# Attention's feature products in 64-column halves, two logits tiles, and a new order for late pieces: linear attention with two MoE layers

## The chip, the cores and the metric

The kernel runs on one core of a Trainium2 chip. The metric is the device time of one execution in microseconds, the median of several runs. The engines are named as in the profile: PE is TensorE, DVE VectorE, ACT ScalarE, POOL GpSimd, SP the engine that issues most DMAs.

## The reference

Three layers follow each other on 1152 tokens (batch 2 x 576 positions) of width 512. The first is linear attention with random features, 8 heads of 64 and 128 features; the second is a feed-forward layer with a clipped activation, whose weights come in 64-bit floats; the third sends each token to the best of 8 experts, at most 288 tokens to each.

```
def phi(x):
    h = einsum('bhsd,md->bhsm', x, omega) - sum(x * x) / 2
    return exp(h - max(h)) / sqrt(m)
kv  = einsum('bhsm,bhsd->bhmd', phi(k), v);  z = sum_s phi(k)
out = einsum('bhsm,bhmd->bhsd', phi(q), kv) / (phi(q) . z + 1e-6)

h = x @ w_in;  y = (h * clip(h + 3, 0, 6) / 6) @ w_out

expert_idx = argmax(y @ w_gate)        # top 1, softmax weight gate_w
out[i] = gate_w[i] * (relu(y[i] @ w1[e]) @ w2[e])   # first 288 tokens of e, others 0
```

## The kernel before

**Attention.** Work is cut into 18 units, listed in `seq`: eight of the keys, eight of the queries (batch x half of the positions x group of heads), and a rest unit of each (`R`, the last 64 positions of both batches). A unit has eight slots of 128 positions, in two halves of four. Its steps have letters: XH and XL split the input into a high and a low part (ScalarE, then GpSimd or VectorE, `halve_x`); B makes the features `pj` on TensorE (`features`, L792); N is the maximum on VectorE (`nm`, L798); P the exponentials on ScalarE (`phi`, L804, one instruction a slot). Key units then do K, `kv_acc`: one product a slot with `phi` as the 128 x 128 stationary operand and 65 columns of the values (`kvp`, L815), accumulated over the four units of a batch. Query units do C and T (`turn_phi`: `tpC` on TensorE, L845, copied to `phT` on ScalarE, L849), D (`attend`: `nd`, four slots a half, L863), R, S, X on VectorE (division), E (`turn_out`: `tpE`, L888), EH and EL (copy and low part of `xT`, L911 and L914). The rest unit's `nd` (L861) already goes in two 64-column halves, since its two batches need different `kvz`.

**First MoE layer.** Each of 16 blocks f of w_in and of w_out arrives as 512 KB of 64-bit words and is turned into 32-bit floats by five operations (L245 to L255): for all blocks in `abs_act` the first is on ScalarE, the others on VectorE. For w_in, ScalarE copies the high part (`wsplit`, L261) and GpSimd subtracts it (L263). The hidden groups `hp` (`hidden_in`, L276, twelve products of 384 columns, 48 groups: 16 f x 3 groups of tokens g) follow, then `t` (ScalarE, L280), `g` (VectorE, L284) and a store to DRAM. The gate is folded into w_out: `tpW` turns a w_out block (L298), `wogp` multiplies it with w_gate (L308). The logits `lg` (`logits`, L330) add `wog` (8 columns) times `g` over f, the three token groups at column tiles 0, 32 and 64 of one bank. In the last six f (`TAIL`) the steps are for token group 0 alone, then for 1 and 2. `logits_out` copies them (`lc`), `turn_logits` turns them (`lgr`, L352 and L355).

**Experts.** The first expert is chosen from the first 384 tokens while the hidden layer still runs. A window of tokens is loaded (`gw`), halved (`gh` on ScalarE L564, the low part on VectorE L566), and multiplied with halved w_out (`yw`, L573) into `dT` (L583 and L585), the input of the expert. The expert's weights arrive in eight loads (`rawe`: four of w1, L605, four of w2, L608) and each is split into two halves, 16 in all (`wsplit`, L618 on ScalarE, then L620 on VectorE and GpSimd in turn); `hp` (L641) is its first product.

**The order.** A planner adds each step with its engine, an estimated cost, a rank, what it comes `after`, and what buffers it `takes` and `frees` (`tp`: four PSUM banks, `pj` two, `acc` one). It simulates the engines, and `DELTA` moves attention's steps by numbers. What comes out is a fixed row of instructions for each engine, which the chip runs in that row; the costs have no other effect. DMA issues on SP are such a row too.

## Time and profile before

| | |
|---|---|
| median of 3 runs | 341.66 us (340.96 to 342.4) |
| profiled execution | 339.61 us, span 337.7 us |
| PE busy | 319.2 us, 95% |
| DVE busy | 226.5 us, 67% |
| ACT busy | 177.7 us, 53% |
| POOL busy | 75.3 us, 22% |

The span goes from the first to the last instruction; the rest of the device time lies around it. Attention's products take about the first 82 us, the first MoE layer runs to 214, the entry of the first expert to 246.5. Busy shares are means over stages with different limits, so the rows further down are by stretch.

### The profile page before, as it was taken

The page shows a single profiled execution, that of the slowest core. Times are in us where ns is not written, and L with a number is a line of the kernel's source. Part 1 is how long each engine was busy: PE and PEld are TensorE (multiplying, and loading weights), DVE is VectorE, ACT ScalarE, POOL GpSimd, SP SyncE. Part 2 cuts the span into 40 slices and gives each one's busy share as a digit, 9 for nine tenths or more (in the row PEclk, how much of TensorE's full clock was granted, in tenths as well). Part 3 has the DMA queues.
Part 4 walks back from the last instruction along what each step waited for, and adds up shares of the span by engine and source line. Part 5 has one row for each costly group of instructions (what it writes and reads, how often), then busy time and mean ns, then how long its engine had stood idle before and what let it go on. Part 6 is the DMA issues. An engine that isn't in the chain of part 4 may idle for free.

```text
span 337.7 us, 6444 instructions
## 1 busy us (share of the span) xinstructions
PE 319.2 (95%) x2311; PEld 291.3 (86%) x2311; DVE 226.5 (67%) x466; ACT 177.7 (53%) x428; POOL 75.3 (22%) x74
## 2 busy tenths in 40 slices
PE   7999899999999998999899999989889999999992
PEld 5999899999989895979687888789789989999782
DVE  5589999898899899979988634269857002835100
ACT  5988899982445464555478223343727132633110
POOL 0755643100131033013100000033406012601021
PEclk9999999999999999999999999999979999999998
DMA  7997940004756868885533142781963006600011
GB/s 247 351 338 271 310 158 32 34 2 171 209 186 214 274 219 258 244 267 199 180 140 118 47 147 73 233 285 45 307 194 127 2 22 186 229 3 0 4 47 31
DMA packets 29673, 54.06 MB, mean 160 GB/s; under 512 B 5536, under 2 KB 18208, under 8 KB 29632
## 3 DMA queue, kind: packets, MB, share of 16 engines
q1 hardware_dynamic: 29248, 52.38, 47.1%
q0 software_dynamic: 384, 1.18, 1.1%
q8 instruction: 20, 0.33, 0.4%
q14 instruction: 21, 0.17, 0.2%
HBM read 37.42 MB, written 16.13 MB: 159 GB/s over the span
## 4 chain that ended last, share of the span: by engine, by line
PE 51%; DMA 16%; DVE 15%; issue 12%; ACT 3%; SPq 1%; POOL 1%; POOLq 0%; ACTq 0%; DVEq 0%
PE hp L276 13%; PE yw L573 8%; PE hp L641 6%; DMA raw<-in_w_in_dram 6%; PE pj L792 6%; PE yq L663 4%; PE nd L863 4%; DMA raw<-in_w_out_dram 4%; PE lg L330 3%; DMA rawe<-in_w_dram 2%; DVE g L284 2%; DVE x L255 2%; PE kvp L815 2%; PE tpC L845 2%; DVE x L253 2%
## 5 line engine op out<-in xcount | busy, mean ns | idle before, releaser
L276 PE MATMUL hp<-xT,wsplit 128*128 128x384 f32 x576 | 107.8, 340 | 0.0
L276 PEld LDWEIGHTS hp<-xT,wsplit 128*128 128x128 f32 x576 | 98.9, 188 | 6.1 <-issue 5.3
L573 PE MATMUL yw<-gh,ohi 128*128 128x288 f32 x256 | 52.1, 298 | 0.2 <-ACT scratch L703 0.2
L280 ACT ACTIVATE t<-hp,three 128x384 f32<-128x384 f32 x48 | 27.7, 578 | 39.2 <-PE hp L276 38.0
L620 POOL TENSOR_TENSOR wsplit<-rawe,wsplit 128x512 fp32r<-128x512 f32 x16 | 22.3, 1394 | 102.2 <-ACT wsplit L618 101.9
L804 ACT ACTIVATE phi<-pj,nm 128x128 f32<-128x128 f32 x144 | 40.6, 415 | 5.9 <-DVE nm L798 4.9
L573 PEld LDWEIGHTS yw<-gh,ohi 128*128 128x128 f32 x256 | 40.9, 188 | 1.6 <-issue 0.6
L263 POOL TENSOR_TENSOR wsplit<-x,wsplit 128x512 fp32r<-128x512 f32 x16 | 21.8, 1360 | 90.3 <-ACT wsplit L261 87.0
L284 DVE SCALAR_TENSOR_TENSOR g<-t,hp 128x384 f32<-128x384 f32 x48 | 26.3, 549 | 19.1 <-ACT t L280 19.0
L566 DVE TENSOR_TENSOR gh<-gw,gh 128x288 fp32r<-128x288 f32 x32 | 19.6, 624 | 29.0 <-ACT gh L564 29.0
L573 PE MATMUL yw<-gh,olo 128*128 128x288 f32 x128 | 37.6, 294 | 0.0
L641 PE MATMUL hp<-dT,wsplit 128*128 128x288 f32 x192 | 27.8, 307 | 3.0 <-DVE dT L585 2.2
L641 PEld LDWEIGHTS hp<-dT,wsplit 128*128 128x128 f32 x192 | 27.2, 198 | 3.2 <-DVE dT L585 2.5
L798 DVE TENSOR_REDUCE nm<-pj 128x4 f32<-128x512 f32 x36 | 24.6, 684 | 4.8 <-PE pj L792 4.0
L782 POOL TENSOR_TENSOR xl<-rawx,xh 128x512 fp32r<-128x512 f32 x16 | 21.6, 1359 | 24.1 <-ACT xh L780 24.1
L792 PE MATMUL pj<-wbd,xh 128*128 128x256 f32 x144 | 25.6, 300 | 1.4 <-ACT xh L780 1.0
L573 PEld LDWEIGHTS yw<-gh,olo 128*128 128x128 f32 x128 | 24.1, 189 | 0.0
L618 ACT ACTIVATE wsplit<-rawe 128x512 fp32r<-128x512 f32 x32 | 19.0, 623 | 8.5 <-DMA rawe<-in_w_dram 8.4
L792 PEld LDWEIGHTS pj<-wbd,xh 128*128 128x128 f32 x144 | 19.5, 190 | 3.2 <-ACT xh L780 2.1
L564 ACT ACTIVATE gh<-gw 128x288 fp32r<-128x288 f32 x32 | 13.5, 438 | 14.1 <-PE yw L573 10.7
L620 DVE TENSOR_TENSOR wsplit<-rawe,wsplit 128x512 fp32r<-128x512 f32 x16 | 16.5, 1031 | 4.2 <-ACT wsplit L618 4.0
L253 DVE SCALAR_TENSOR_TENSOR x<-raw,x 128x512 int32<-128x512 int32 x16 | 18.7, 1170 | 0.4
(150 smaller groups left out, 481.5 us busy)
## 6 DMA issues: line engine op xcount, KB each, us to landing
gall<-g SPq DMA_DIRECT2D x48, 192.0 KB, 2.4
...
```

The source lines that it names most:

```text
L253: nc.vector.scalar_tensor_tensor(out=x, in0=lw, scalar=29, in1=x, op0=ALU.logical_shift_right, op1=ALU.bitwise_or)
L263: nc.gpsimd.tensor_tensor(out=t[:, 1, :], in0=xf, in1=t[:, 0, :].bitcast(F32), op=ALU.subtract)
L276: nc.tensor.matmul(hp, lhsT=w[:, a, wk], rhs=xT[g][b_][:, kk, :], start=(n == 0), stop=(n == 3 * KD - 1))
L280: nc.scalar.activation(out=t, in_=hp, func=ACTF.Relu, bias=three[:, 0:1])
L284: nc.vector.scalar_tensor_tensor(out=gv, in0=t, scalar=6.0, in1=hp, op0=ALU.min, op1=ALU.mult)
L573: nc.tensor.matmul(self.ps[kk], lhsT=wohalf[f][a][:, kk * 128:(kk + 1) * 128], rhs=self.gh[f][:, b_, :], start=(f == YORDER[0] and n == 0) ...
L620: engine.tensor_tensor(out=lo, in0=part, in1=hi.bitcast(F32), op=ALU.subtract)
L641: nc.tensor.matmul(hp, lhsT=self.w[0, f][:, a, kk * 128:(kk + 1) * 128], rhs=self.window.dT[b_][:, kk, :], start=(n == 0), stop=(n == 3 * ...
L782: (nc.gpsimd if u in X_POOL else nc.vector).tensor_tensor(out=lo[:, sl], in0=rawt[u][:, sl], in1=hi[:, sl].bitcast(F32), op=ALU.subtract)
L792: nc.tensor.matmul(pj[:, 2 * jj:2 * jj + 2, :], lhsT=a[:, j, :], rhs=w, start=(jj == 0 and n == 0), stop=(n == 2), skip_group_check=True,)
L798: nc.vector.tensor_reduce(out=nm, in_=pj, axis=AX.X, op=ALU.max, negate=True)
L804: nc.scalar.activation(out=phis[u][:, 4 * half + h, :], in_=pj[:, h, :], func=ACTF.Exp, bias=nm[:, h:h + 1])
```

## The change

Five things are changed.

1. `kv_acc` takes a whole unit in one step, and each slot's product is made in two halves of 64 columns of `phi` (`CH`), which land in partitions 0 to 63 and 64 to 127. `attend_products` does the same for `nd`: one step D0 a unit of sixteen products, with two `tp` banks taken at once, after both `phT` halves. `C` of a unit comes after D0 of the unit two before it.
2. `DELTA` has other numbers, the planner some other costs, and hidden groups from the seventh on come after all of attention.
3. For the eight late w_in blocks (`abs_act`, f 8 to 15) the low part of `wsplit` is subtracted on VectorE in place of GpSimd.
4. `wog` has 32 columns. In the tail the odd f of a pair goes to another column tile (3, 0 and 3 for groups 0, 1 and 2), so that two rows of weights are worked on at once; `summed` adds the two tiles when the logits are turned. The copy is one for all 128 partitions in each of the two parts, the first turning is now three products like the second, and the clearing of the scratch (`lz`) is gone.
5. The first expert's loads go out as w2 0 to 2, w1 0 to 3, w2 3, the first three without waiting for the window loads. The save of the second part's `meta` comes after the last window load.

```
-        nc.gpsimd.tensor_tensor(out=t[:, 1, :], in0=xf, in1=t[:, 0, :].bitcast(F32), op=ALU.subtract)
+        (nc.vector if key in abs_act else nc.gpsimd).tensor_tensor(out=t[:, 1, :], in0=xf, in1=t[:, 0, :].bitcast(F32), op=ALU.subtract)
...
-        wog[b] = const.tile([128, BLOCK, E], F32, name=f"wog{b}")
-        nc.scalar.activation(out=wog[b], in_=tp[:, :, 0:E], func=ACTF.Copy)
+        wog[b] = const.tile([128, BLOCK, 32], F32, name=f"wog{b}")
+        nc.scalar.activation(out=wog[b], in_=tp, func=ACTF.Copy)
...
         for f in fs:
             for g in gs:
+                other = f % 2 > 0 and len(gs) < NG
+                ct = {0: 3, 1: 0, 2: 3}[g] if other else g
                 nc.tensor.matmul(
-                    lg[0][32 * g:32 * g + E, :], lhsT=wog[f // BLOCK][:, f % BLOCK, :], rhs=gt[f, g],
-                    start=(f == 0), stop=(f == F1T - 1), skip_group_check=True,
+                    lg[0][32 * ct:32 * ct + 32, :], lhsT=wog[f // BLOCK][:, f % BLOCK, :], rhs=gt[f, g],
+                    start=(f == 0 or (other > 0 and f == F1T - TAIL + 1)), stop=(f >= F1T - PAIR), skip_group_check=True,
                 )
...
-    def logits_out(g):
-        ps = slice(32 * g, 32 * g + E)
-        nc.scalar.activation(out=lgT[0][ps], in_=lg[0][ps], func=ACTF.Copy)
+    def logits_out(p):
+        if not p:
+            lgT[0] = scratch()[:, 0:GT]
+        nc.scalar.activation(out=lgT[0], in_=lg[0], func=ACTF.Copy)
...
-        if p == 0:
-            for c in range(TPG):
-                nc.tensor.transpose(lgr[p][:, c, :], lgT[0][0:E, c * 128:(c + 1) * 128], ident[0:E, 0:E])
-            return
         for c in range(TPG):
-            nc.tensor.matmul(
-                lgr[p][:, c::TPG, :], lhsT=lgT[0][:, c * 128:(c + 1) * 128],
-                rhs=ident.rearrange("p (g e) -> p g e", e=32)[:, 1:NG, 0:E], start=True, stop=True,
-            )
+            nc.tensor.matmul(lgr[p][:, c::TPG, :], lhsT=lgT[0][:, c * 128:(c + 1) * 128], rhs=summed[:, p:2 * p + 1], start=True, stop=True)
...
+        for g, (a, b) in enumerate(((0, 3), (1, 0), (2, 3))):
+            nc.gpsimd.tensor_tensor(out=summed[:, g], in0=tiles[:, a], in1=tiles[:, b], op=ALU.add)
...
+    def kv_acc(b, u, first, last):
...
+        for s in range(8):
             h, r = slot_head(u, s)
-            nc.tensor.matmul(
-                kv_ps[b][:, h, r:r + D + 1], lhsT=phis[u][:, s, :], rhs=vt[:, h, r * (D + 1):(r + 1) * (D + 1)],
-                start=first and s == 0, stop=last, skip_group_check=True,
-            )
+            for c in CH:
+                nc.tensor.matmul(
+                    kv_ps[b][c, h, r:r + D + 1], lhsT=phis[u][:, s, c], rhs=vt[:, h, r * (D + 1):(r + 1) * (D + 1)],
+                    start=first and s == 0, stop=last, skip_group_check=True,
+                )
...
+    def attend_products(u):
+        b = seq[u][1]
+        phT = phTs[u]
+        for half in range(2):
+            nds[u, half] = pt.tile([128, 4, 128], F32, tag="tp", name="nd")
+        for s in range(8):
+            h, r = slot_head(u, s)
+            for n, c in enumerate(CH):
+                nc.tensor.matmul(nds[u, s // 4][c, s % 4, 0:D + 1], lhsT=phT[:, s, c], rhs=kvz[n if b == "R" else b][:, h, 1:D + 2])
...
+        plan.add(
+            f"D0{u}", "PE", 1.2, lambda u=u: attend_products(u), after=[f"T0{u}", f"T1{u}"] + [f"KV{bb}" for bb in range(B) if b in (bb, "R")],
+            takes=[("tp", f"D{z}{u}") for z in range(2)], frees=[f"T0{u}"], rank=rank("D", u))
...
-            (f"H{me}", "PE", 2.09, dict(after=[f"WLi{f}"] + rows_of(g), takes=tag, frees=[f"wi{f}"] + ([f"x{g}0", f"x{g}1"] if f == F1T - 1 else []), rank=n)),
+            (f"H{me}", "PE", 2.09, dict(after=[f"WLi{f}"] + rows_of(g) + (attended if n >= 6 else []), takes=tag, frees=[f"wi{f}"] + ([f"x{g}0", f"x{g}1"] if f == F1T - 1 else []), rank=n)),
...
+        if k == 0:
+            parts = parts[F2T // 2:-1] + parts[:F2T // 2] + parts[-1:]
+        for n, (kind, h) in enumerate(parts):
+            early = k == 0 and n < F2T // 2 - 1
+            load2(f"e{k}.{kind}{h}", lambda a=(kind, h): x.load(*a), 2.0, 2.5, after=[f"ce{k}"] + ([] if early else [f"Lgw{k}.{min(F1T - 1, 4 * n + 3 - 10 * (k == 0))}"]), takes="raww", rank=-1900 + n + 400 * k,
```

How the rows of instructions move, at three places. An entry is a line of the kernel (two or three lines off between the two), an operation, its output and inputs and its shape; names are those of the code.

TensorE, the end of attention, before: the last `nd` groups, each of a half unit, stand in a row with `tpE` and `tpC`, and the first hidden group (L276) follows.

```order
L792 MATMUL pj<-wbd_140,xh 128x256 x2
L792 MATMUL pj<-wbd_141,xh 128x256 x2
L792 MATMUL pj<-wbd_140,xl 128x256 x2
L861 MATMUL nd<-kvz,phT 64x65 x8
L863 MATMUL nd<-kvz,phT 128x65 x8
L888 MATMUL tpE<-ident,x 128x128 x4
L845 MATMUL tpC<-ident,phi 128x128 x8
L888 MATMUL tpE<-ident,x 128x128 x4
L276 MATMUL hp<-xT_93,wsplit 128x384
```

The same place after, from the last but two `tpE` on:

```order
L891 MATMUL tpE<-ident,x 128x128 x4
L847 MATMUL tpC<-ident,phi 128x128 x4
L790 MATMUL pj<-wbd_141,xh 128x256 x2
L790 MATMUL pj<-wbd_142,xh 128x256 x2
L790 MATMUL pj<-wbd_141,xl 128x256 x2
L863 MATMUL nd<-kvz,phT 64x65 x16
L847 MATMUL tpC<-ident,phi 128x128 x4
L277 MATMUL hp<-xT_94,wsplit 128x384
```

A unit's `nd` is one row of sixteen products (L863), behind the features of the last unit, and a hidden group (L277) stands behind the next `tpC`. Some rows later, where that hidden group ends:

```order
L277 MATMUL hp<-xT_94,wsplit 128x384
L891 MATMUL tpE<-ident,x 128x128 x4
L847 MATMUL tpC<-ident,phi 128x128 x4
L863 MATMUL nd<-kvz,phT 64x65 x32
L277 MATMUL hp<-xT_96,wsplit 128x384
```

The last two units' `nd` (32 products) follow the last `tpC`, and another hidden group stands ahead of the last `tpE`; three hidden groups stand before it in this stretch, two before the change.

VectorE, where a late block of w_in is decoded (`x_` with a number), before:

```order
L284 SCALAR_TENSOR_TENSOR g<-t,hp 128x384
L249 TENSOR_SCALAR x_1709<-x_1709 128x512
L251 TENSOR_SCALAR x_1709<-x_1709 128x512
L253 SCALAR_TENSOR_TENSOR x_1709<-raw,x_1709 128x512
L284 SCALAR_TENSOR_TENSOR g<-t,hp 128x384
L255 SCALAR_TENSOR_TENSOR x_1709<-raw,x_1709 128x512
L249 TENSOR_SCALAR x_1749<-x_1749 128x512
L251 TENSOR_SCALAR x_1749<-x_1749 128x512
```

And after:

```order
L254 SCALAR_TENSOR_TENSOR x_1787<-raw,x_1787 128x512
L285 SCALAR_TENSOR_TENSOR g<-t,hp 128x384
L256 SCALAR_TENSOR_TENSOR x_1787<-raw,x_1787 128x512
L250 TENSOR_SCALAR x_1821<-x_1821 128x512
L252 TENSOR_SCALAR x_1821<-x_1821 128x512
L264 TENSOR_TENSOR wsplit<-x_1787,wsplit 128x512
L285 SCALAR_TENSOR_TENSOR g<-t,hp 128x384
L254 SCALAR_TENSOR_TENSOR x_1821<-raw,x_1821 128x512
L256 SCALAR_TENSOR_TENSOR x_1821<-raw,x_1821 128x512
```

The low part of a block (L264) now stands on VectorE between two steps of the next block's decoding.

ScalarE, from the last hidden groups' `t` to the copy of the last logits (`scratch<-lg`), before:

```order
L280 ACTIVATE t<-hp,three 128x384 x5
L564 ACTIVATE gh<-gw 128x288 x3
L280 ACTIVATE t<-hp,three 128x384 x4
L343 ACTIVATE scratch<-lg 8x384 x2
L564 ACTIVATE gh<-gw 128x288 x4
L618 ACTIVATE wsplit<-rawe 128x512 x2
L564 ACTIVATE gh<-gw 128x288
L618 ACTIVATE wsplit<-rawe 128x512 x2
```

And after:

```order
L281 ACTIVATE t<-hp,three 128x384 x5
L562 ACTIVATE gh<-gw 128x288 x2
L281 ACTIVATE t<-hp,three 128x384
L562 ACTIVATE gh<-gw 128x288
L281 ACTIVATE t<-hp,three 128x384
L616 ACTIVATE wsplit<-rawe 128x512 x2
L281 ACTIVATE t<-hp,three 128x384
L616 ACTIVATE wsplit<-rawe 128x512 x2
L281 ACTIVATE t<-hp,three 128x384
L616 ACTIVATE wsplit<-rawe 128x512 x2
L344 ACTIVATE scratch<-lg 128x384
L562 ACTIVATE gh<-gw 128x288 x6
```

Six weight halves of the first expert (L616, of w2) now stand between the last `t`, ahead of the copy; before, the first two stood behind it. VectorE ahead of the first expert's `dT`, before:

```order
L1061 TENSOR_TENSOR have<-have,inside_3219 128x9
L1064 TENSOR_REDUCE left<-have 128x1
L1067 CAST leftb<-left 128x1
L620 TENSOR_TENSOR wsplit<-rawe,wsplit 128x512
L628 TENSOR_SCALAR tok<-slotidx,st_3137 96x3
L630 SCALAR_TENSOR_TENSOR tok<-sm,we_3117,tok 96x3
L633 TENSOR_SCALAR to<-tok 96x3
L620 TENSOR_TENSOR wsplit<-rawe,wsplit 128x512
L566 TENSOR_TENSOR gh<-gw,gh 128x288 x3
L585 SCALAR_TENSOR_TENSOR dT_3332<-yw,dT_3331 128x288 x4
```

And after:

```order
L618 TENSOR_TENSOR wsplit<-rawe,wsplit 128x512
L564 TENSOR_TENSOR gh<-gw,gh 128x288
L1061 SCALAR_TENSOR_TENSOR inside_3364<-meta,we_3263,inside_3364 128x9
L1063 TENSOR_TENSOR have<-have,inside_3364 128x9
L1066 TENSOR_REDUCE left<-have 128x1
L1069 CAST leftb<-left 128x1
L564 TENSOR_TENSOR gh<-gw,gh 128x288 x3
L1075 CAST lefti<-lp 128x1
L583 SCALAR_TENSOR_TENSOR dT_3462<-yw,dT_3461 128x288 x4
```

Before, two weight subtracts (L620) stand in the last seven rows ahead of `dT`; after, the nearest one (L618) is eight rows away, and the window halves (L564) remain.

## Rows read from the trace of the kernel before

**Rows 1.** Busy us (and instructions) by stretch; columns named in the first line.

```profile
core 0: us, PE busy (x) PEld busy (x) DVE busy (x) ACT busy (x) POOL busy (x), PEclk, DMA share, GB/s
40.00:70.00 30.00, 30.00 (x276) 29.59 (x275) 27.50 (x67) 28.58 (x90) 10.17 (x8) 1.00 0.24 82
82.00:162.00 80.00, 77.47 (x543) 69.20 (x541) 72.43 (x122) 41.03 (x79) 15.92 (x12) 1.00 0.74 229
162.00:214.00 52.00, 51.05 (x310) 40.79 (x310) 33.59 (x83) 23.29 (x46) 0.70 (x2) 1.00 0.34 118
214.00:246.50 32.50, 28.02 (x215) 26.96 (x215) 23.70 (x67) 16.19 (x37) 9.45 (x7) 1.00 0.66 211
```

**Rows 2.** The same view in stretches of 10 us: attention's start, the first expert's entry.

```profile
10.00:20.00 10.00, 9.81 (x84) 9.60 (x84) 6.48 (x11) 10.00 (x37) 8.72 (x18) 1.00 0.94 331
...
240.00:250.00 10.00, 7.05 (x40) 6.68 (x40) 7.85 (x20) 5.13 (x13) 2.69 (x2) 0.83 0.66 215
```

**Rows 3.** Chain of waits, in attention: start us, us, what.

```profile
36.57 0.84 PE kvp L815 x8
37.41 1.79 PE nd L863 x16
...
67.69 0.62 PE nd L861 x16
68.31 0.58 PE tpC L845 x4
...
69.33 0.44 PE tpC L845 x4
```

**Rows 4.** Timeline of ACT, 64 to 73 us: start us, us, operation, count.

```profile
66.66 2.20 ACT L804 ACTIVATE phi<-pj,nm 128x128 f32<-128x128 f32 x8
...
69.95 0.62 ACT L849 ACTIVATE phT<-tpC 128x512 f32<-128x512 f32 x1
```

**Rows 5.** Chain of waits, around the last logits.

```profile
163.61 1.40 PE lg L330 x12
165.01 2.30 PE hp L276 x12
...
167.75 2.09 PE hp L276 x12
...
170.27 1.39 PE lg L330 x4
...
184.11 2.68 PE lg L330 x8
...
194.10 1.39 PE lg L330 x8
```

**Rows 6.** The tile `lgr`: count, ns min/median/max, first and last start.

```profile
L355 PE MATMUL lgr<-ident,scratch x6: 178/262/263, 221.9 to 222.4; 128*128 128x16 f32 x6
L352 PE MATMUL lgr<-ident,scratch x3: 201/202/223, 189.0 to 189.2; 8*128 8x8 f32 x3
```

**Rows 7.** Waits of PE, 80 to 170 us, and timelines of DVE and POOL.

```profile
PE tpW L298 <- DVE wo L255: 3.0, 3, 1.4
...
119.38 0.68 DVE L255 SCALAR_TENSOR_TENSOR x<-raw,x 128x512 int32<-128x512 int32 x1
...
120.89 1.75 DVE L253 SCALAR_TENSOR_TENSOR x<-raw,x 128x512 int32<-128x512 int32 x1
...
161.25 1.65 DVE L255 SCALAR_TENSOR_TENSOR wo<-raw,wo 128x512 int32<-128x512 int32 x1
...
120.80 1.29 POOL L263 TENSOR_TENSOR wsplit<-x,wsplit 128x512 fp32r<-128x512 f32 x1 [15.53 <-ACT wsplit L261]
```

**Rows 8.** PE waits from 214 us, DVE before `dT`, the tile `rawe`.

```profile
PE hp L641 <- DVE dT L585: 2.2, 1, 2.2
...
244.88 1.19 DVE L566 TENSOR_TENSOR gh<-gw,gh 128x288 fp32r<-128x288 f32 x3
...
L620 DVE TENSOR_TENSOR wsplit<-rawe,wsplit x16: 677/692/1781, 222.4 to 309.6; 128x512 fp32r<-128x512 f32 x16
...
DMA to landing us min/median/max: 3.3/5.0/6.6
```

89 lines of the change are left out of this document (36 added, 53 removed).

## The prediction

> **What bounds the kernel now.** I read the busy shares of the page first (the table above), then busy time by stage, then the chain of waits inside each stage, then the waits of the engine that the chain stays on. TensorE is the busiest by far, and by stage it is the same: 30.00 of 30 us in the middle of attention, 77.47 of 80 and 51.05 of 52 in the first MoE layer, 28.02 of 32.5 at the entry of the first expert [rows 1]. So a cheaper TensorE instruction is worth its full difference wherever no second engine is full too, and the places with a second full engine are what the reader should look for: ScalarE is busy 28.58 of 30 us in the middle of attention [rows 1] and 10.00 of 10 at its start [rows 2]. VectorE has 72.43 of 80 in the stretch where the first MoE layer's weights are decoded [rows 1]; it is near its limit, but TensorE still wins there. The entry of the first expert is the one stage where TensorE waits, 4.5 of 32.5 us, and the 10 us at its end ran at a mean granted clock of 0.83 [rows 2].
>
> The profiled execution took 339.61 us, 2.05 below the median of 341.66. I sum differences: from the profiled execution they lead to a time 2.05 lower than the one I give, which stands against the median.
>
> **A, products of attention in halves of 64 columns.** The price of a half-width product is in the trace already, since the rest unit's `nd` is written that way: sixteen records, four slots in two halves, take 0.62 us, while four slots at full width (eight records) take 0.84 [rows 3]. What comes after pays: the `tpC` behind the half-width group took 0.58, an undisturbed one 0.44 [rows 3], so 0.14 for the change of shape. A unit of `kvp` (two calls of 0.84, 1.68) becomes 2 x 0.62 + 0.14 = 1.38, 0.30 less; a unit of `nd` (1.79 for sixteen records [rows 3]) becomes 1.38, 0.41 less. Eight units of each: 2.4 + 3.3, and the rest unit, whose two halves now stand together, pays one change less, 0.1. Together 5.8. That is one end.
> What of it reaches the end? The first four `kvp` units stand where ScalarE is full [rows 2]; there TensorE only waits longer: 1.2 off, 4.6 left. In the stretch from 40 to 70 us ScalarE has 1.4 us to spare [rows 1], and the change takes nothing from ScalarE; with 1.4 as the whole gain one has the other end. But TensorE needn't idle there: the new order puts three hidden groups of the MoE layer ahead of the last `tpE`, where two stood (the rows of the order for this place show the third one's neighbours), and one such group is 2.09 us [rows 5] that no longer has to be done later. 1.4 + 2.1 and half a microsecond for the units on either side of the stretch make 4.0, nearer to the upper end. **A = -4.0, bounds -1.4 and -5.8.**
> The Trainium skill ("TensorEngine Tiling (Array Packing)", section Theoretical Speedup) gives up to 2 times for a dimension of at most 64. By that a unit would take half, A would be up to 13.9 and the whole sum up to 20.4; the rest unit's row shows 0.84 against 0.62, which is 1.35 times, and the sum goes by the row.
>
> **B, last logits on two column tiles.** A round of logits, three 8-column tiles side by side, takes 0.70: twelve records in 1.40, two rounds [rows 5]. In the tail the steps are for one group of tokens or for two, so tiles stand empty: one one-group step takes 1.39, the next two, which stand together, 2.68, and each of three two-group steps 1.39 or more [rows 5]. With the odd row of weights on a tile of its own each step is one round: 1.39 - 0.70, 2.68 - 1.40 and 3 x 0.70 make 4.1. The turning of the first logits grows from three small transposes, 0.3, to the same six records that the second takes today, 0.7 [rows 6]: 0.4 back. TensorE is at 51.05 of 52 here, and hidden groups follow that wait for nothing, so the gain stays. The other bound: after a logits step the next hidden group takes 2.30 instead of 2.09 [rows 5]; if four tiles make entry and exit dearer by as much again at the five places of the tail, 2.1 more goes. **B = -3.7, bounds -1.6 and -4.1.**
>
> **C, late subtracts from GpSimd to VectorE.** Eight `wsplit` subtracts of 1.29 us leave GpSimd. The VectorE operation that runs beside each is stretched: 1.75 at 120.89 and 1.65 at 161.25, where one of the same kind a moment before took 0.68 [rows 7]. Over the eight (the first and the last are shown) the excess is 8.5 us. On VectorE a subtract of this size takes 0.69 as a median and 1.78 at worst [rows 8], so 5.5 for eight: VectorE comes out 2.9 us shorter. What TensorE sees of it are its waits for decoded w_out words at `tpW`: 3.0 us in three waits, the longest 1.4 [rows 7], and the two long ones end right behind stretched operations. With both gone it is 2.7; with each of the three longer by one subtract of 0.69, which now stands in the same queue ahead of those words, it is +2.1. I take a value on the side of the gain, since VectorE's total falls, but under half of it, since TensorE's idle time here is small and a later wait may follow: **C = -1.0, bounds -2.7 and +2.1.**
>
> **D, first expert's loads.** Three of the four w2 loads go out before w1, and the new order makes six of the sixteen weight halves on ScalarE ahead of the window product, in a stretch where VectorE has 33.59 of 52 [rows 1]. Today TensorE waits 2.2 us for `dT` on VectorE [rows 8]; ahead of `dT` VectorE has two weight subtracts (one of them stretched) and three window halves, 1.19 [rows 8]. In the new order no weight subtract stands in the seven rows ahead of `dT`; the three window halves still do. One of them, 0.4, I leave standing in the way: 2.2 - 0.4, **D = -1.8**. Upper end: the whole wait and what a clock of 0.83 costs in 10 us, 1.7 [rows 2]: -3.9. Lower end: those six splits sit in ScalarE's queue between the last `t`, which VectorE and then TensorE need soon; a load lands after 5.0 as a rule and 6.6 at worst [rows 8], 1.6 late, with everything behind it held: +1.6.
>
> **E, the rest**: the order table elsewhere, the planner's costs, the wider `wog` (its load into the array is one load as before), one copy of logits for two, three small GpSimd adds for `summed`, the save of `m1` behind the window loads. Each is work on an engine that waits in its stretch: nothing.
>
> Sum: -4.0 - 3.7 - 1.0 - 1.8 = -10.5; 341.66 - 10.5 = **331.2 us**.
>
> **Rivals.**
> R1, ScalarE sets the end of attention: it is the second full engine [rows 1, 2], nothing is taken from it, and the retuned order may only shift the idle time. A is 0, the rest stays: 335.2. For it speaks 28.58 of 30; against it the third hidden group in front.
> R2, changes of shape cost more than in the one unit that shows them. Suppose each group of halves pays 0.21 on entry and on exit, as a hidden group behind logits does [rows 5], in place of 0.14 once: `kvp` keeps almost nothing and `nd` 0.13 x 8, A = -1.0; B is at its small end, -1.6; C and D give nothing: 339.1. The Trainium skill (same page, Key Properties) says that changing the tiling mode drains TensorE, and the change makes some two dozen more such changes; the rows price one at 0.14 or 0.21.
> R3, the other side: `nd` of a unit now waits for both turned halves of `phi` and takes two of the four `tp` banks at once, so that `tpC`, `tpE` and every second hidden group have two left. If nothing else is at hand, TensorE waits for ScalarE's second `phT` (0.62) and half of a `phi` batch of 2.20 ahead of it in the queue [rows 4]: 1.7 in each of nine units, 15.4, and the time is 346.6. From (343.4 - 331.2) / 9 = 1.36 a unit on the kernel is slower by what can be told. Against it: the order puts `pj` groups or a whole hidden group between `tpC` and `nd`.
> R4, every term at its good end: 5.8 + 4.1 + 2.7 + 3.9 = 16.5, 325.2.
> R5, a half costs half: the pairs run wholly side by side and four slots take 0.42 in place of 0.84 [rows 3]. A is up to 8 x 0.84 + 8 x 0.90 = 13.9, and the time 331.2 + 4.0 - 13.9 = 321.3. Against it stand the 0.62 of the rest unit and ScalarE's full stretches; a small chance. (It is what the skill's figure under A would give.)
>
> **How the numbers follow.** Forecast 0.53 (327.5 to 335), R1 0.17 (333.5 to 337.5), R2 0.09 (337 to 341), R3 0.09 (342 to 347), R4 0.10 (323.5 to 327), R5 0.02. A range from 325.0 to 339.0 leaves out R3, R5, half of R2 and a third of R4, in all 0.19. A measurement of this kernel can tell about 0.5% from no change, that is 339.95 and 343.4. Faster: 0.53 + 0.17 + 0.10 + 0.02 and 0.05 of R2 = 0.87; within: 0.04 of R2 and 0.01 of R3 = 0.05; slower: 0.08.
>
> **What the profile after would show.** A: a unit of `kvp` or `nd` in 1.25 to 1.4, and all later hidden groups some 4 us earlier; if the units are that cheap but the last `tpE` is no earlier and TensorE shows gaps released by ScalarE, it is R1; if the `tpC` and `pj` behind them take more than 0.14 extra, R2; if `nd` has idle time released by `phT`, R3; units of 0.84 are R5. B: tail steps of 0.70. C: no VectorE operation of 1.6 us where the late w_in tiles are decoded, and the waits of `tpW` gone. D: the first hidden group of the first expert close behind the window product, the wait for `dT` under half a microsecond, and the clock of that slice nearer to 1. The prediction fails if the half-width groups of `kvp` don't run side by side as the rest unit's `nd` does, or if a new gap opens at the start of attention, where loads land and ScalarE is full.

## The result and the profile after

The changed kernel takes 332.9 us (332.38 to 333.3) where the kernel before takes 342.03 (340.96 to 342.5) beside it: a ratio of 0.974, 95% interval 0.971 to 0.977. Measured a second time it was 332.39 against 340.5, 0.976 (0.972 to 0.980). The profiled execution took 332.73 us with a span of 330.9, 6.8 less than the span of before.

Busy time by stretch, as in [rows 1, 2] (the first three lines are the start of attention, the fourth its middle, the last the first expert's entry; the stretch from 82 to 174 us is the decoding). The columns are those of [rows 1].

```profile
10.00:20.00 10.00, 9.36 (x141) 8.68 (x142) 6.75 (x11) 10.00 (x36) 8.63 (x19) 1.00 0.96 347
20.00:30.00 10.00, 6.37 (x49) 5.48 (x47) 9.76 (x15) 8.04 (x27) 4.62 (x5) 1.00 0.96 317
30.00:35.00 5.00, 4.47 (x46) 3.99 (x48) 3.35 (x8) 3.88 (x13) 3.84 (x3) 0.66 0.43 173
40.00:70.00 30.00, 28.56 (x386) 26.31 (x385) 29.32 (x72) 28.60 (x90) 8.79 (x7) 1.00 0.35 116
82.00:174.00 92.00, 85.41 (x597) 75.27 (x597) 82.76 (x149) 50.24 (x96) 5.66 (x4) 1.00 0.64 202
240.00:250.00 10.00, 9.61 (x72) 9.32 (x71) 6.12 (x15) 5.69 (x14) 1.29 (x1) 1.00 0.61 207
```

The kernel before had, from 20 to 30 us and in the decoding:

```profile
20.00:30.00 10.00, 9.56 (x83) 9.27 (x82) 9.01 (x18) 8.99 (x29) 3.69 (x3) 1.00 0.97 341
82.00:174.00 92.00, 88.52 (x609) 77.63 (x608) 83.52 (x141) 46.92 (x90) 16.63 (x13) 1.00 0.70 221
```

The first column after the length is TensorE's busy time. Its idle time in the middle of attention went from 0 to 1.4 us, in the decoding from 3.5 to 6.6, and at the first expert's entry the slice that ran at a clock of 0.83 now runs at 1.00. A new gap opened at the start of attention, which the prediction names among its signs of failing: from 20 to 30 us TensorE is idle for 3.6 us, before 0.4. The slice behind it runs at a granted clock of 0.66, which is 1.7 us lost, as much as the slice at the first expert's entry lost before. In a second profiled execution of the changed kernel the gap is there again, the slice behind it runs at 1.00, and a slice at 110 us, behind a wait at `tpW`, runs at 0.66.

TensorE's waits over the whole span (engine, line, waited for: us in total, times, longest); those of before for `tpW` and `dT` are in [rows 7, 8], the one for `phi` stands last here.

```profile
PE pj L790 <- ACT phi L802: 5.7, 8, 1.9
PE tpW L299 <- DVE wo L256: 5.3, 4, 2.0
PE wogt L318 <- ACT wogT L315: 1.2, 1, 1.2
...
PE lg L334 <- DVE g L285: 1.1, 1, 1.1
...
PE hp L639 <- DVE dT L583: 0.4, 1, 0.4
```

```profile
PE pj L792 <- ACT phi L804: 0.4, 1, 0.4
```

Three of the eight waits for `phi`, 4.1 us of the 5.7, end between 23 and 31 us. The chain of waits there (start us, us, what) leads over VectorE, whose maximum `nm` stands behind steps of the decoding:

```profile
25.61 0.61 DVE x L254
26.25 1.65 DVE x L256
...
28.62 0.69 DVE nm L796
...
29.60 0.89 ACT phi L802 x3
...
30.53 1.26 PE pj L790 x6
```

And the chain of waits at the places of [rows 3] and [rows 5]:

```profile
54.14 1.08 PE kvp L817 x32
55.22 0.59 PE tpC L847 x4
56.52 1.08 PE nd L863 x32
...
59.34 0.44 PE tpC L847 x4
...
170.98 0.77 PE lg L334 x4
...
184.20 1.42 PE lg L334 x8
...
193.09 0.78 PE lg L334 x8
```

The reader should see two things together. The operations themselves became cheaper than the prediction said: a whole unit of `kvp` or `nd` takes 1.08, and with the 0.15 that the next `tpC` takes longer 1.23, not 1.38. A step of the logits' tail takes 0.77, near the 0.70 foretold (the two one-group steps together 1.42). And yet new waits stand in the list: 5.7 us for `phi`, 5.3 for decoded words at `tpW`. Where the 6.8 us of the span came from can be followed by three marks in the timelines (us from the span's start):

| mark | before | after | difference |
|---|---|---|---|
| 34th hidden group's `t` on ScalarE | 174.0 | 174.1 | +0.1 |
| first window product `yw` | 213.9 | 212.3 | -1.6 |
| first `yq` of the first expert | 260.8 | 254.1 | -6.7 |
| end | 337.7 | 330.9 | -6.8 |

Attention and decoding together won nothing in this execution, the tail 1.7, and the first expert's entry 5.1. In the second profiled execution they won 0.6, 2.1 and 5.1.

### The profile page after: what moved, and what is told of

It is laid out like the page before. It is cut to its first block, busy times and chain, and to the rows that moved or that the text cites. A ratio compares the mean times of both kernels' runs of the same rounds, so it can differ in the third digit from the quotient of the medians.

```text
span 330.9 us, 6974 instructions
## 1 busy us (share of the span) xinstructions
PE 306.9 (93%) x2570; PEld 278.7 (84%) x2570; DVE 222.3 (67%) x474; ACT 177.5 (54%) x427; POOL 65.4 (20%) x68
## 4 chain that ended last, share of the span: by engine, by line
PE 51%; DVE 15%; DMA 15%; issue 9%; ACT 4%; POOL 2%; SPq 1%; POOLq 0%; ACTq 0%; DVEq 0%
PE hp L277 14%; PE yw L571 14%; PE hp L639 6%; DMA raw<-in_w_in_dram 4%; PE yq L661 4%; PE pj L790 4%; DMA raw<-in_w_out_dram 3%; PE nd L863 3%; DVE nm L796 2%; DMA rawe<-in_w_dram 2%; PE lg L334 2%; DMA out_dram<-scratch,to 2%; DVE g L285 2%; DMA rawx<-in_k_dram 2%; DVE x L252 2%
## 5 line engine op out<-in xcount | busy, mean ns | idle before, releaser
L277 PE MATMUL hp<-xT,wsplit 128*128 128x384 f32 x576 | 107.8, 340 | 0.0
L277 PEld LDWEIGHTS hp<-xT,wsplit 128*128 128x128 f32 x576 | 98.9, 188 | 5.1 <-issue 5.0
L618 POOL TENSOR_TENSOR wsplit<-rawe,wsplit 128x512 fp32r<-128x512 f32 x16 | 22.0, 1379 | 160.6 <-ACT wsplit L616 141.6
L564 DVE TENSOR_TENSOR gh<-gw,gh 128x288 fp32r<-128x288 f32 x32 | 18.0, 578 | 30.1 <-ACT gh L562 27.8
L790 PE MATMUL pj<-wbd,xh 128*128 128x256 f32 x144 | 26.3, 305 | 6.5 <-ACT phi L802 5.7
L639 PE MATMUL hp<-dT,wsplit 128*128 128x288 f32 x192 | 26.3, 296 | 0.4 <-DVE dT L583 0.4
L639 PEld LDWEIGHTS hp<-dT,wsplit 128*128 128x128 f32 x192 | 25.7, 188 | 0.6 <-DVE dT L583 0.6
L616 ACT ACTIVATE wsplit<-rawe 128x512 fp32r<-128x512 f32 x32 | 19.0, 622 | 1.3 <-DMA rawe<-in_w_dram 1.1
L264 POOL TENSOR_TENSOR wsplit<-x,wsplit 128x512 fp32r<-128x512 f32 x8 | 11.6, 1450 | 29.9 <-ACT wsplit L262 29.9
L689 PE MATMUL yp<-wsplit,h 128*96 128x512 f32 (+1 forms) x96 | 16.9, 337 | 0.0
L689 PEld LDWEIGHTS yp<-wsplit,h 128*96 128x96 f32 x96 | 13.5, 162 | 3.4
```

Of the source, the lines that this page charges most:

```text
L277: nc.tensor.matmul(hp, lhsT=w[:, a, wk], rhs=xT[g][b_][:, kk, :], start=(n == 0), stop=(n == 3 * KD - 1))
L616: nc.scalar.activation(out=hi, in_=part, func=ACTF.Copy)
L618: engine.tensor_tensor(out=lo, in0=part, in1=hi.bitcast(F32), op=ALU.subtract)
L639: nc.tensor.matmul(hp, lhsT=self.w[0, f][:, a, kk * 128:(kk + 1) * 128], rhs=self.window.dT[b_][:, kk, :], start=(n == 0), stop=(n == 3 * ...
L689: nc.tensor.matmul(ps_, lhsT=self.h2[f // 4, a][:, f % 4, c * SR:(c + 1) * SR], rhs=self.w[1, f][:, b_, x * w:(x + 1) * w], start=(n == 0) ...
L790: nc.tensor.matmul(pj[:, 2 * jj:2 * jj + 2, :], lhsT=a[:, j, :], rhs=w, start=(jj == 0 and n == 0), stop=(n == 2), skip_group_check=True,)
```

## The experiments

Two theories stood at the start. Theory 1 is the prediction's sum: TensorE sets the time and each part counts by itself. Theory 2 came from the marks above: TensorE's saved time ahead of the decoding runs into waits, and most of the gain is made at the first expert. The kernels are each compared with the kernel before on the same chip; a difference between two of them is the difference of the ratios times 340.5 us, the median of before there. The measure for the kernels with one part undone is the second measurement of the changed kernel, 0.976.

### The changed kernel again

> The changed kernel itself, beside the single parts and on their chip. Every theory expects its ratio again, 0.974 of before (0.971 to 0.977); it is the measure for the kernels with one part undone.

Measured: 332.39 us, 0.976 (0.972 to 0.980). Its trace has waits at `tpW` of 3.3 us where the first had 5.3, so single waits vary by some 2 us from one execution to the next.

### One part undone in the changed kernel

The halves at full width again:

```
-            for c in CH:
-                nc.tensor.matmul(
-                    kv_ps[b][c, h, r:r + D + 1], lhsT=phis[u][:, s, c], rhs=vt[:, h, r * (D + 1):(r + 1) * (D + 1)],
+            nc.tensor.matmul(
+                kv_ps[b][:, h, r:r + D + 1], lhsT=phis[u][:, s, :], rhs=vt[:, h, r * (D + 1):(r + 1) * (D + 1)],
...
+            if b != "R":
+                nc.tensor.matmul(nds[u, s // 4][:, s % 4, 0:D + 1], lhsT=phT[:, s, :], rhs=kvz[b][:, h, 1:D + 2])
+                continue
```

> The changed kernel with kvp and nd (not the rest unit's) at full width again, same steps, banks and order. Theory 1 (the sum of the prediction: TensorE sets the time, each part counts by itself): the time rises by term A, about 4.0 us (1.4 to 5.8), and if the traces' cheaper units count in full, 12.9 us (kvp 15.7 busy against 9.2, nd 17.4 against 11.0). Theory 2 (VectorE's decoding sets the stretch from 82 to 174 us, and TensorE's time saved ahead of it runs into waits): the added 12.9 us of TensorE work fill its waits of today in attention (about 6) and in decoding (about 6.5), and the time rises by 0 to 2 us.

Measured: 0.995 (0.989 to 1.001), 6.6 us slower than the changed kernel: above theory 2's 0 to 2, below theory 1's 12.9, a little above the predicted term's upper end. A part of it is no product at all. Columns as in [rows 1]:

```profile
25.00:30.00 5.00, 3.00 (x22) 2.35 (x20) 4.84 (x8) 4.17 (x13) 1.71 (x1) 1.00 0.92 330
30.00:35.00 5.00, 3.60 (x25) 3.61 (x26) 4.40 (x10) 4.24 (x14) 3.06 (x2) 0.84 0.64 245
35.00:40.00 5.00, 5.00 (x25) 5.00 (x25) 1.91 (x6) 2.76 (x7) 4.39 (x5) 0.50 0.69 256
40.00:45.00 5.00, 5.00 (x32) 5.00 (x30) 2.72 (x5) 2.31 (x8) 1.30 (x2) 0.64 1.00 302
```

TensorE waits 3.4 us of the first ten (two waits for `phi`), and the granted clock falls to 0.50, the lower of its two levels, in the third slice, where TensorE is busy throughout. The slices lose 0.8, 2.5 and 1.8 us of clock, 5.1 in this execution, where the changed kernel's profile lost 1.7 behind the same gap. So this undoing prices the halves together with a clock that most of its executions lose (the mean clock is 0.973 to 0.983 in eleven of twelve, 0.990 in the fastest, which took 335.7), and it can't be read as the price of the halves.

One tile for two of the three pairs of the tail:

```
-                other = f % 2 > 0 and len(gs) < NG
+                other = f == F1T - TAIL + 1 and len(gs) < NG
...
```

> The changed kernel with only the first of three pairs of the logits' tail on two column tiles, the other two pairs on one tile as before; order unchanged. Theory 1: two thirds of 4.1, the time rises by 2.8 us. Theory 2: the traces show that from the 34th hidden group (174 us in both) to the window product only 1.6 us were won, and that the last logits wait 1.1 us for VectorE's g; the four slower steps add 2.8 of TensorE work, the wait of 1.1 hides a part, the time rises by 1.0 to 1.7 us.

Measured: 0.982 (0.977 to 0.988), 2.2 us slower. Its interval overlaps that of the changed kernel, and it lies between the two expectations: no verdict for either.

The late subtracts on GpSimd again:

```
-        (nc.vector if key in abs_act else nc.gpsimd).tensor_tensor(out=t[:, 1, :], in0=xf, in1=t[:, 0, :].bitcast(F32), op=ALU.subtract)
+        nc.gpsimd.tensor_tensor(out=t[:, 1, :], in0=xf, in1=t[:, 0, :].bitcast(F32), op=ALU.subtract)
...
-                (f"WL{nm}", *(("DVE", 0.6) if (kd, f) in abs_act else ("Pool", 1.25)), dict(after=[f"w{nm}"], frees=[f"W0{nm}"], rank=n if (kd, f) in abs_act else -300)),
+                (f"WL{nm}", "Pool", 1.25, dict(after=[f"w{nm}"], frees=[f"W0{nm}"], rank=-300)),
```

> The changed kernel with the eight late subtracts of wsplit on GpSimd again. Theory 1: the time rises by term C, 1.0 us (-2.1 to +2.7). Theory 2 (VectorE sets the decoding): VectorE becomes 2.9 us longer in that stretch (8.5 us of stretched operations against eight subtracts of 0.69), the time rises by 2 to 3 us, and the waits of tpW grow by as much.

Measured: 0.988 (0.982 to 0.994), 4.1 us slower. That is more than the predicted term's 1.0 and above its other end, 2.7. TensorE's waits at `tpW` grew to 6.9 us, the longest 3.1, and the two slices of 5 us from 125 us on, where that one falls, ran at 0.72 and 0.60, 3.4 us of clock. So here too wait and clock are priced together.

The first expert's loads in the old order:

```
-        parts = [(kind, h) for kind in range(2) for h in range(F2T // 2)]
-        if k == 0:
-            parts = parts[F2T // 2:-1] + parts[:F2T // 2] + parts[-1:]
-        for n, (kind, h) in enumerate(parts):
-            early = k == 0 and n < F2T // 2 - 1
-            load2(f"e{k}.{kind}{h}", lambda a=(kind, h): x.load(*a), 2.0, 2.5, after=[f"ce{k}"] + ([] if early else [f"Lgw{k}.{min(F1T - 1, 4 * n + 3 - 10 * (k == 0))}"]), takes="raww", rank=-1900 + n + 400 * k,
-                  then=["Le{}.{}{}".format(k, *parts[n - 1])] if n else [])
-        for n, (kind, f) in enumerate((kind, 2 * h + a) for kind, h in parts for a in range(2)):
+        for n, (kind, h) in enumerate((kind, h) for kind in range(2) for h in range(F2T // 2)):
+            load2(f"e{k}.{kind}{h}", lambda a=(kind, h): x.load(*a), 1.46, after=[f"ce{k}"] + [f"Lgw{k}.{min(F1T - 1, 4 * n + 3)}"], takes="raww", rank=-1900 + n + 400 * k)
+        for n, (kind, f) in enumerate((kind, f) for kind in range(2) for f in range(F2T)):
```

> The changed kernel with the first expert's loads in the old order (w1 0 to 3, w2 0 to 3, all after window loads). Theory 1: the time rises by term D, 1.8 us. Theory 2: the traces put 3.6 us of the gain between the start of the window product and the first expert's hidden group, and 1.6 us more behind it, where the clock of 0.83 is gone; the time rises by 4 to 5.5 us, the wait for dT comes back (about 2 us) and a 10 us slice behind it shows a clock near 0.83.

Measured: 0.997 (0.993 to 1.001), 7.0 us slower. The wait for `dT` is back at 2.1, and so is the clock of 0.83:

```profile
PE yw L571 <- DVE gh L564: 2.5, 2, 1.6
PE hp L639 <- DVE dT L583: 2.1, 1, 2.1
```

```profile
240.00:250.00 10.00, 8.25 (x51) 8.28 (x52) 5.04 (x13) 2.03 (x6) 0.00 (x0) 0.83 0.65 204
```

The first of these waits is new: the window product of the second expert waits 2.5 us for `gh`, in neither the kernel before nor the changed kernel. So the 7.0 holds more than the first expert's entry.

The four undone parts cost 6.6, 2.2, 4.1 and 7.0 us, 19.9 together, where the whole change is worth 8.2. A part of the excess is the clock and the new wait just named; beyond that, parts in the changed kernel support each other, or something else in the change costs time. The next kernels ask this from the other side.

### One part alone in the kernel before

The halves, inside the old half-unit steps, banks and order:

```
-            nc.tensor.matmul(
-                kv_ps[b][:, h, r:r + D + 1], lhsT=phis[u][:, s, :], rhs=vt[:, h, r * (D + 1):(r + 1) * (D + 1)],
+            for c in CH:
+                nc.tensor.matmul(
+                    kv_ps[b][c, h, r:r + D + 1], lhsT=phis[u][:, s, c], rhs=vt[:, h, r * (D + 1):(r + 1) * (D + 1)],
...
-                nc.tensor.matmul(nd[:, z, 0:D + 1], lhsT=phT[:, s, :], rhs=kvz[b][:, h, 1:D + 2])
+                for c in CH:
+                    nc.tensor.matmul(nd[c, z, 0:D + 1], lhsT=phT[:, s, c], rhs=kvz[b][:, h, 1:D + 2])
```

> The kernel before with part A alone: kvp and nd in 64-column halves inside the old half-unit steps, the old banks, waits and order. Theory 1 (each part counts by itself): 4.0 us faster (1.4 to 5.8), and TensorE's units of half a unit take about 0.6 us (or 0.54, half of the 1.08 that a whole unit takes in the changed kernel) in place of 0.84. Theory 2 (ScalarE and VectorE set attention and decoding, TensorE's saved time becomes waits): the busy time of kvp and nd falls by 10 us or more, TensorE's waits in attention and at tpW grow by nearly as much, and the time falls by 0 to 2 us.

Measured: 0.996 (0.993 to 0.999), 1.3 us faster. This is theory 2's number. The profile fell on the slowest of the twelve executions, 341.09 us, whose span is 1.5 us longer than that of before; it shows where time goes in attention, and not the gain of the median. TensorE's chain, its waits, and its busy time up to the end of attention's last `tpE` (the first of the two lines is the kernel before):

```profile
54.27 0.61 PE kvp L818 x16
54.88 0.59 PE tpC L848 x4
```

```profile
PE pj L792 <- ACT phi L804: 3.0, 8, 0.7
...
PE rk L431 <- DVE ohb L420: 2.5, 1, 2.5
```

```profile
0.00:81.89 81.89, 78.20 (x659) 74.34 (x660) 68.12 (x150) 67.75 (x205) 30.68 (x39) 1.00 0.55 191
0.00:80.12 80.12, 73.21 (x915) 63.23 (x916) 67.63 (x150) 67.40 (x205) 30.60 (x39) 1.00 0.56 196
```

A half unit takes 0.61 or 0.62, as the rest unit's rows said, and the `tpC` behind it 0.59. Taken by themselves, the groups of `kvp` and `nd` fall from 33.0 to 21.5 us, the 10 and more that theory 2 expected. But neighbouring groups overlap, and the `tpC` behind a group of halves is longer: TensorE as a whole is busy 5.0 us less in attention. Its idle time there grows by 3.2 us, with 3.0 of waits for `phi` (0.4 before), so attention ends 1.8 us earlier. Waits of nearly 10 us, as theory 2 had them, are not there. At the window product 1.6 us of the 1.8 are left. Behind the window product this execution loses more than that: the routing of the second part makes TensorE wait 2.5 where it waited 1.0, and the two slices of 5 us behind the wait for `dT` run at 0.60 and 0.71, where before only one was below 1.00, at 0.66.

The loads, the new order of the first expert's weights in the kernel before (the lines of `add_weights` as in the change's diff):

> The kernel before with part D alone: the first expert's loads as w2 0 to 2, w1 0 to 3, w2 3. Theory 1: 1.8 us faster (up to 3.9). Theory 2 (undoing D cost 8 us in the changed kernel, of which only 5 are in the trace's waits and clock): 5 to 7 us faster, the wait for dT below half a microsecond and no slice at 0.83 behind it.

Measured: 0.985 (0.980 to 0.990), 5.1 us faster, with no wait for `dT` on VectorE among TensorE's waits (one of 1.0 on ScalarE remains) and a clock of 1.00 in the slice:

```profile
240.00:250.00 10.00, 8.94 (x66) 8.58 (x66) 6.43 (x18) 6.17 (x16) 1.10 (x1) 1.00 0.93 299
```

The late subtracts on VectorE (the `nc.vector if key in abs_act` line and its plan, in the kernel before):

> The kernel before with part C alone: the eight late subtracts on VectorE. Theory 1: 1.0 us faster (-2.7 to +2.1). Theory 2 (VectorE sets the decoding): VectorE's busy time falls by 3 to 4 us, and the time by 2 to 4, with the waits of tpW shorter than 3.0.

Measured: 0.990 (0.985 to 0.995), 3.5 us faster. TensorE's wait at `tpW` is 0.3 us, and it is busy 91.39 of 92 in the decoding:

```profile
PE tpW L298 <- DVE wo L255: 0.3, 1, 0.3
```

```profile
82.00:174.00 92.00, 91.39 (x630) 81.04 (x629) 80.52 (x148) 46.68 (x88) 5.82 (x5) 1.00 0.72 226
```

The window product starts 3.9 us earlier. VectorE's whole busy time fell from 226.5 to 224.0, by 2.5 and not the 3 to 4 of theory 2. The span of this execution is only 1.2 us shorter than that of before. The wait for `dT` (2.2 as before) now has two slices of 5 us at a low clock around it, where before there was one, at 0.66:

```profile
240.00:245.00 5.00, 2.46 (x9) 2.25 (x10) 4.34 (x14) 1.48 (x5) 0.00 (x0) 0.73 0.46 137
245.00:250.00 5.00, 5.00 (x25) 5.00 (x25) 1.61 (x3) 1.45 (x3) 0.00 (x0) 0.59 0.74 227
```

The tail on two tiles, with the copy and the turning (the lines of `logits`, `logits_out` and `turn_logits` as in the change's diff):

> The kernel before with part B alone: logits of 32 columns, the tail on two column tiles, one copy of logits, turning with the summed constant. Theory 1 (each part counts by itself): 3.7 us faster (1.6 to 4.1). Theory 2 (a gain counts only where TensorE sets the time up to the next wait): the trace of the changed kernel wins 1.6 us between the 34th hidden group and the window product, so 1.5 to 2.5 us faster, and the rest comes back as a wait for the last g or for the second routing.

Measured: 0.990 (0.986 to 0.995), 3.2 us faster; the window product starts 3.0 us earlier. That is nearer to theory 1's number than to theory 2's, whose 1.5 to 2.5 the interval (1.6 to 4.9 us) doesn't leave out.

### All four parts in the kernel before, and the rest of the change

The four parts alone give 1.3, 3.2, 3.5 and 5.1 us, 13.1 together. The change as a whole gave 8.2. So a third theory: the rest of the change, which the prediction put at nothing, costs some 4 us. The rest is the table of numbers, the whole-unit steps with their two banks, the hidden groups held back from the seventh on, the other planner's costs, and the later save of `meta`.

> The kernel before with all four parts, halves, tail, late subtracts and loads, but its own table of numbers, its half-unit steps and its costs. The parts alone gave -0.8, -3.0 and -5.1 us, and the tail some -2. Theory 1 (parts add up, and the rest of the change, the new numbers and whole-unit steps, is worth nothing): about 332, the changed kernel's ratio of 0.975. Theory 3 (the new numbers and whole-unit steps make the decoding later: hidden groups 10 to 12 start 2 to 4.5 us after those of the kernel before, although attention ends earlier): faster than the changed kernel by 2 to 4 us, 328 to 330, a ratio of 0.963 to 0.969, and hidden groups 10 to 34 start ahead of those of the kernel before.

Measured: 327.95 us, 0.968 (0.962 to 0.975), 10.8 us faster than the kernel before, so the parts add up to within the noise. That is 2.6 us faster than the changed kernel by the ratios, whose intervals overlap, and 4.4 by the medians. The span is 324.8, against 330.9 and 330.3 of the changed kernel's two profiled executions, and the 10th to 34th `t` start 0.1 to 6.4 us before those of the kernel before, where the changed kernel's start 0.1 to 5.0 us after them. TensorE waits for no decoded word at all:

```profile
PE pj L790 <- ACT phi L802: 3.3, 8, 1.0
```

```profile
82.00:174.00 92.00, 91.41 (x632) 81.67 (x631) 79.36 (x147) 47.45 (x89) 5.59 (x4) 1.00 0.71 228
```

Is it the table of numbers?

```
-    DELTA = {'consts': 172.4, 'XH0': 7.9, 'XL0': 162.8, 'OM': 17.4, 'OL': -135.3, 'B0': -35.7, 'N0': -102.4, 'P0': 43.4, 'XH1': 5.0, 'XL1': -25.3, 'B1': -28.8, 'N1': -83.0, 'P1': 52.0, 'XH2': 412.1, 'XL2': -95.8, 'B2': -8.2, 'N2': 67.1, 'P2': -3.7, 'KT': 274.4, 'K0': -8.3, 'KW': 141.3, 'KV': -15.6, 'K1': 15.7, 'C1': 127.6, 'T1': 91.1, 'D1': 17.2, 'R1': 27.8, 'S1': -0.4, 'X1': 178.6, 'E1': 182.5, 'EH1': 45.1, 'EL1': -150.5, 'C2': -8.8, 'T2': 158.1, 'D2': 96.9, 'R2': 12.6, 'S2': 129.1, 'X2': 17.9, 'E2': -20.4, 'EH2': 146.6, 'EL2': -87.9, 'KR': -30.3}
+    DELTA = {'consts': 73.6, 'XH0': 2.2, 'XL0': 79.9, 'OM': -2.4, 'OL': 8.1, 'B0': 30.5, 'N0': 0.2, 'P0': -1.8, 'XH1': -26.1, 'XL1': -0.3, 'B1': -16.4, 'N1': -0.1, 'P1': 160, 'XH2': 242.5, 'XL2': -48.2, 'B2': 19.5, 'N2': -20.7, 'P2': 116.6, 'KT': 26.7, 'K0': 32.4, 'KW': 57.3, 'KV': 2.3, 'K1': 26.6, 'C1': 119.2, 'T1': 28.1, 'D1': 59.8, 'R1': -21.7, 'S1': 4, 'X1': 54.7, 'E1': 135.3, 'EH1': -15.4, 'EL1': -36.5, 'C2': -14.6, 'T2': 72.2, 'D2': 141.5, 'R2': 3.8, 'S2': 3.7, 'X2': 40.7, 'E2': -69.9, 'EH2': 16.5, 'EL2': -6.5}
```

> The changed kernel with the old table of numbers for attention's order, all else as changed. Theory 1: 0 (term E). Theory 3: with the old numbers the decoding starts as early as before and the time falls by 2 to 4 us. A third case: the old numbers don't suit whole-unit steps that take two banks at once, TensorE waits for ScalarE in attention by more than the 6 us of the changed kernel, and the time rises.

Measured: 0.982 (0.976 to 0.988), 2.1 us slower than the changed kernel, with intervals that overlap; the waits at `tpW` are 3.7 us. The old numbers don't bring the time back. The waits for `phi` are about as long in sum, 5.4 us in ten waits, so it isn't the third case either; but the longest is 0.9, where the changed kernel has 1.9, and no slice at the start of attention runs below 1.00.

Then the order in which decoded words are used. In the changed kernel VectorE's decoding is ahead of that of the kernel before (43 of its 140 operations are done at 82 us, 35 before; the last one is at 163 us, 171 before), and TensorE waits for it all the same. The timelines show why; first TensorE, then VectorE (start us, us, operation, count, idle time before and what ended it):

```profile
101.06 0.66 PE L299 MATMUL tpW<-ident,wo 128*128 128x128 f32 x4 [1.70 <-DVE wo L256]
...
111.10 0.63 PE L299 MATMUL tpW<-ident,wo 128*128 128x128 f32 x4 [2.00 <-DVE wo L256]
```

```profile
107.93 0.69 DVE L254 SCALAR_TENSOR_TENSOR wo<-raw,wo 128x512 int32<-128x512 int32 x1
109.80 0.55 DVE L285 SCALAR_TENSOR_TENSOR g<-t,hp 128x384 f32<-128x384 f32 x1 [1.18 <-ACT t L281]
110.27 0.68 DVE L256 SCALAR_TENSOR_TENSOR wo<-raw,wo 128x512 int32<-128x512 int32 x1
```

At 111 TensorE stands at a `tpW` until the last step of that block (110.27) is done. That step stands in VectorE's row behind a `g`, for which VectorE itself waited 1.2 us. The rows of TensorE show the move: the fifth `tpW` stands behind 9 hidden groups in the changed kernel and behind 12 in the kernel before. The planner's costs can explain it: with decoding planned at 0.34 and 0.60 us a step (the traces show 0.42 and 0.69), a `tpW` seems ready earlier. The last kernel undoes these costs alone:

```
-            for j, cost in enumerate((0.34, 0.34, 0.34, 0.6, 0.6))
+            for j, cost in enumerate((0.43, 0.43, 0.43, 0.69, 0.69))
...
-            steps[0] = (steps[0][0], "ACT", 0.52, dict(after=[f"Vw{n}"], rank=n - 600))
+            steps[0] = (steps[0][0], "ACT", 0.62, dict(after=[f"Vw{n}"], rank=n - 600))
```

> The changed kernel with one thing of its planner's costs undone: the five decoding steps are planned at 0.43, 0.43, 0.43, 0.69, 0.69 us again (the first on ScalarE 0.62), not 0.34, 0.34, 0.34, 0.60, 0.60 (0.52). Costs set only the order: TensorE's tpW then stand later between the hidden groups. Theory 4 (what the rest of the change costs is that tpW stand in TensorE's row before their words are decoded): waits of tpW below 1.5 us (5.3 and 3.3 in the two looks at the changed kernel, none with the old costs in the kernel with all four parts), the last hidden group 3 to 5 us earlier, 328 to 330 us, a ratio of 0.962 to 0.970. If the whole-unit steps or the table of numbers are to blame: the waits remain or move to pj, and the ratio stays at 0.974 to 0.976.

Measured: 329.29 us, 0.967 (0.963 to 0.971), 3.2 us faster than the changed kernel. The fifth `tpW` now stands behind 10 hidden groups. The time is as theory 4 expected, two of its signs are not: TensorE's waits at `tpW` are 2.4 us, the longest 1.0, not below 1.5, and not far from the 3.3 of the changed kernel's second profile. The one at `wogt` is gone:

```profile
PE tpW L299 <- DVE wo L256: 2.4, 4, 1.0
```

```profile
82.00:174.00 92.00, 88.92 (x615) 77.88 (x614) 80.29 (x150) 48.70 (x93) 5.77 (x4) 1.00 0.69 214
```

TensorE's idle time in the decoding falls from 6.6 (4.7 in the second profile) to 3.1 us, and the last hidden group is 2.3 to 3.0 us earlier, not 3 to 5. The waits for `phi` fell too, from 5.7 and 6.6 to 4.3. So it is shown that the five costs lose 3.2 us; that they lose it at `tpW` is shown for a part of it only. With all four parts and the old half-unit steps the idle time in the decoding is 0.6. By the ratios these two kernels are level; what lies between their traces was not told apart. One piece can be named from the profiles: the gap at the start of attention is still there in the last kernel (TensorE busy 1.95 us from 25 to 30 us, the next 5 us at a clock of 0.66), and it is not there with all four parts in the kernel before (4.29, and 1.00).

## Why the prediction was right, and where its terms were not

The forecast of 331.2 us and the way it went were right, but four of its five terms were off, in ways that cancelled: that the sum came out so near is luck. Parts alone, measured in the kernel before, with the interval of the ratio in us (E is the changed kernel against the four parts together):

| term | predicted, bounds | alone | undone in the changed kernel |
|---|---|---|---|
| A halves | -4.0, -1.4 to -5.8 | -1.3, -0.2 to -2.4 | +6.6, with a clock loss of 5.1 |
| B logits' tail | -3.7, -1.6 to -4.1 | -3.2, -1.6 to -4.9 | +2.2 (two thirds of it) |
| C late subtracts | -1.0, -2.7 to +2.1 | -3.5, -1.6 to -5.3 | +4.1, with a clock loss of 3.4 |
| D first loads | -1.8, -3.9 to +1.6 | -5.1, -3.6 to -6.7 | +7.0, with a wait of 2.5 elsewhere |
| E rest | 0 | +2.6 to +4.4 (by ratios, by medians) | -3.2 (decoding costs alone) |

**A.** The step from the rest unit's rows was right for a half unit (0.62 measured, and 0.59 for the `tpC` behind it) and too shy for a whole one: 1.08, not two times 0.62 and an exit. The failing step is the next one, "1.4 + 2.1 and half a microsecond". The third hidden group does start before the last `tpE`, as foretold, but that `tpE` ends at 82.1 us where it ended at 81.9, and TensorE waits for `phi` (5.7 us where it was 0.4). In the kernel before the halves come to 1.3 us. By the prediction's own signs that is R1, priced at 0.17, for this term, but ScalarE is not the only full neighbour: VectorE is busy 29.32 of 30 us in the middle of attention, where it had 27.50 [rows 1], and 9.76 of 10 from 20 to 30 us, where ScalarE has 8.04 and the chain leads over VectorE's `nm`. For attention the prediction weighed ScalarE alone. Which of the two engines sets the middle of attention was not tested. The long waits at the start of attention, 4.1 of the 5.7 us, come with the new table of numbers and not with the halves: full-width products in the new order have them too (1.4 and 2.0), the halves alone have no wait for `phi` above 0.7, and the changed kernel with the old table none above 0.9. R3 didn't come: no wait of `nd` for `phT` stands among TensorE's waits, and R2 and R5 are out, at 0.59 for the next `tpC` and 1.08 a unit.

**B.** Right, with its sum: 0.77 for a step that was 1.39, 1.42 for two that were 2.68. In the changed kernel one piece of it is lost at the very end, by a mishap close to D's lower bound (from the timelines of VectorE, ScalarE and TensorE):

```profile
209.62 1.36 DVE L618 TENSOR_TENSOR wsplit<-rawe,wsplit 128x512 fp32r<-128x512 f32 x1 [0.56 <-ACT wsplit L616]
209.69 0.58 ACT L281 ACTIVATE t<-hp,three 128x384 f32<-128x384 f32 x1
210.90 0.54 DVE L285 SCALAR_TENSOR_TENSOR g<-t,hp 128x384 f32<-128x384 f32 x1
211.50 0.83 PE L334 MATMUL lg<-g,wog 128*32 128x384 f32 x2 [1.07 <-DVE g L285]
```

It is not ScalarE's splits that hold the last `t`: it starts as the last hidden group ends. The subtract of a w2 half on VectorE holds the last `g`, for some 0.6 us, and the last logits wait 1.1 us for it. In the second profile this wait is 0.7, and with the tail alone 0.5.

**C.** The mechanism was right (VectorE un-stretched, 2.5 us shorter against 2.9 expected, the waits at `tpW` from 3.0 to 0.3), the value was not. The failing step is "under half of it, since TensorE's idle time here is small and a later wait may follow". Up to the window product no later wait followed: the waits at `tpW` fell by 2.7, the whole of what I had called the best end, and TensorE's idle time in the decoding from 3.5 to 0.6 us. The window product came 3.9 us earlier; the last microsecond of these isn't in any wait and stays unplaced. Behind it the profiled execution gave most of this back, 1.7 us of it in clock, so that the 3.5 rests on the median and not on this trace.

**D.** Right in kind, a third of the size. The wait for `dT` went from 2.2 to 0.4, as foretold. The term was mis-sized because the clock was kept for the upper end and the routing was not looked at. The slice at 0.83 behind that wait belongs to it: without the wait (in the changed kernel and with the loads alone) the slice runs at 1.00, and with the old order of loads both are back. With the loads alone the waits for `dT` on both engines fall from 2.9 to 1.0, the clock gives 1.7, and the wait of 1.0 for the routing (`rk`) is gone: 4.6 us, which is what this trace wins between the first window product and the first `yq` (42.3 us against 46.9). In the changed kernel the clock won here was lost again elsewhere, 1.7 us in either profile.

**E.** Put at nothing, since each piece "is work on an engine that waits", and that is the step that failed most plainly. A planner's cost takes no time, but it moves rows, and a row that is too early makes its engine wait with everything behind it. Five of the costs lose 3.2 us, a part of it at `tpW`. The new table also opened the gap at the start of attention, which was among the prediction's signs of failing and had no price in any term. What else of the rest costs time stays open.

So a sum of -10.5 met -8.2 to -9.1, and its range held, since C and D gave 5.8 us more than forecast, A 2.7 and B 0.5 less, and the rest cost 2.6 to 4.4. Nothing in the prediction's working made these errors cancel.
